# Attention backward on one core: the planner's greedy work order gives way to a fixed cyclic table

## The chip, the cores and the metric

One core of one Trainium2 chip runs the kernel. The metric is the device time of the whole program in microseconds (us); smaller is better. The core's engines are named as the profile names them: PE (TensorE, matrix products; PEld is its weight load), DVE (VectorE), ACT (ScalarE), POOL (GpSimd) and SP (SyncE, which here does nothing but issue transfers). All large transfers go through SP's one queue, all small ones through POOL's. One program stands for each engine, and each engine goes through its own in order: an instruction whose inputs are not there holds up everything behind it on that engine.

## The reference

```python
def _fwd_reference(q, k, v):            # q: 32 x 32 heads x 4 x 128, k and v: 32 x 4 heads x 2048 x 128, bf16
    k = jnp.repeat(k, 8, axis=1)
    v = jnp.repeat(v, 8, axis=1)
    scores = jnp.einsum("bhqd,bhkd->bhqk", q, k) * D ** -0.5
    p = softmax(scores, axis=-1)
    return jnp.einsum("bhqk,bhkd->bhqd", p, v)

def reference(q, k, v, grad_out):
    out, vjp = jax.vjp(_fwd_reference, q, k, v)
    return (out, *vjp(grad_out))        # out, dq, dk, dv
```

It is the forward pass of grouped attention (eight query heads share a key head) and its gradients to q, k and v. For a batch, four key heads with 2048 keys each are read (2 MB of k and 2 MB of v) and gradients of the same sizes are written (2 MB of dk and 2 MB of dv); q, grad_out, out and dq are 32 KB each.

## The kernel before, in words

The 32 batches are independent. With 8 heads x 4 queries, the 32 query rows of each of the four key heads fill the 128 partitions, so that one batch is worked on as a whole. The work of a batch is cut into **units**, made by `units_of` (L125) and turned into instructions by `emit` (L468); the names are those of the code:

- `LQ` loads q and grad_out (POOL's queue, L473 and L475); `LK` and `LV` load one head of k or v, 512 KB each (SP's queue, L481).
- `QT`, `KT`, `VT` (L484, L485, L495) transpose q, grad_out and blocks of k and v on PE, eight 128x128 blocks in a unit; `QTe`, `KTe`, `VTe` copy the result from PSUM to SBUF, on ACT (L463) or DVE (L466).
- `S` (L506) makes scores; `MX` (L513, DVE) the running maximum; `EX` (L522, ACT) the exponentials; `L` (L526, L528) the sums and their reciprocals; `dop`, `qp`, `rs` (POOL, L531 to L538) the scaled small operands.
- `ET` (L546) transposes the exponentials, `O` (L557) makes the output, `Oe` evicts it and `Os` stores it; `DL` (L572) is the row sum of out times grad_out.
- `DP` (L506) makes the gradient of p, `DS` (L579, DVE) that of the scores; `DT` (L546) transposes it, `DQ` (L557) makes dq, `DQe` and `DQs` evict and store it.
- `DV` and `DK` (L594) make four quarters of dv and dk each; every quarter is evicted by two `DVe` or `DKe` (L599), on ACT or DVE, 128x1024 elements each; `DVs` and `DKs` (L603) store two halves of 1 MB through SP's queue, when all four quarters of a half are there.

So a batch gives SP twelve transfers: eight loads of 512 KB and four stores of 1 MB. PE does all its work in three forms: transposes (128x128), products tiled by columns (`S`, `DP`, `O`, `DQ`) and products tiled by rows (`DV`, `DK`).

PSUM is one tile of eight banks (L454); a unit holds one bank or a pair, and `bank_of` says which. SBUF tiles come from pools whose sizes stand in `CAP` (L36): 12 tiles of k, 11 of v, 9 and 6 of the transposed ones, 6 halves of output.

What stands behind what is decided on the host, before the program is built. `plan` (L201) replays the machine: an event queue with occupancies (`OCC`), an instruction-fetch term of PE (`pe_length`, L229) and a transfer queue. Whenever an engine is free in this replay, `begin` (L287) takes the ready unit with the smallest due time, which is `b * PERIOD + DUE[name][i]` plus a correction of its own for batches 0, 1, 29, 30 and 31 (L134). Evictions go to ACT or DVE, whichever ends first (L388 to L403); banks are taken as they are free (`banks_for`, L261); SP takes a store when one is ready, and two loads behind each store if there are any (L378 to L387). The resulting list is emitted in its order (L606), and so each engine's program is the greedy replay's order frozen.

```python
        when = b * PERIOD + due[name[0]][i] + BY_BATCH.get(b, {}).get(name[0], [0.0] * 8)[i]
```

Of the kernel before, what the change touches and what calls it, by code (L numbers as in the profile page):

```python
# [18 lines left out]
NQ = 4  # L19
# [3 lines left out]
OCC = dict(QT=0.16, KT=0.45, VT=0.45, ET=0.45, DT=0.45, S=0.228, DP=0.228, O=0.23, DQ=0.23, DV=0.24, DK=0.24,  # L23
           MX=1.27, EX=1.11, L=0.5, DL=0.28, DS=1.21, dop=0.4, qp=0.4, rs=0.3,
           c16=(0.60, 0.48), c32=(1.135, 0.905), q16=(0.27, 0.165), o32=(0.28, 0.27))
# [3 lines left out]
FETCH, QUEUE, FIRST, EVERY = 2.35, 64, 705, (768, 1024)  # L29
SWITCH = 0.06  # L30
MODE = dict(S=1, DP=1, O=1, DQ=1, DV=2, DK=2)
LAG = dict(PE=0.21, ACT=0.13, DVE=0.13, POOL=0.13)
ISSUE = dict(LQ=1.5, Os=0.75, DQs=0.75)
SERVICE = dict(LQ=0.19, LK=1.287, LV=1.287, DVs=2.574, DKs=2.574, Os=0.18, DQs=0.18)
DMA_LAT, AGAIN, LOAD_LAG, STORE_LAG, AHEAD, HEAD = 2.1, 0.35, 1.4, 1.7, 3.3, 0.8
CAP = dict(q=4, et=2, dt=2, k=12, v=11, kt=9, vt=6, out=6, e=2, ds=2)  # L36
PERIOD = 38.14
FIRST_LQ, EVERY_LQ = -121.38, 29.52
DUE = dict(
    LQ=[2], LK=[-32.2, -26.2, -23.3, -21.6], LV=[-13.6, -7.1, -12.8, -13.3], QT=[379.6], QTe=[276.9],  # L40
    KT=[-1.5, -10.9, 87.6, 39.5, -176.9, 28.1, -28.4, 222.7],
    KTe=[175.1, 41.5, 163.9, 367.8, 163, 50, 155.9, -312],
    VT=[-443.5, -82.7, -68.7, -188.9, 19.6, -41.4, -1.1, 323.7],
    VTe=[323.5, -134.3, -108.5, 190.8, -22.8, 143.9, 133.3, 364.7], S=[219.2, -491.6, -275.5, -226.2],
    MX=[-66.7, -116.8], EX=[-189, 16.2], L=[-9.8], dop=[55.8], qp=[-129], rs=[335.3], ET=[-631.9, -72.5],
    ETe=[86.4, 62.9], DT=[12.5, -272.2], DTe=[309.7, 80.5], O=[-58.1, -99.1, 16, 18.9], Oe=[60.7],
    Os=[-204.4], DQ=[104.1, 202.1, 189, -53.5], DQe=[11.6], DQs=[-172.1], DL=[14.9],
    DP=[-151.2, 118.2, -290.9, -95.2], DS=[-316.3, -308.3], DV=[-207.6, -55.7, -6.3, 43.4],
    DVe=[81.8, 244.9, 385.7, 166.5, -349.8, 322.2, 15.6, -40.9], DVs=[-108.9, -1.7],
    DK=[121.5, 185, -172.9, -271.1], DKe=[-24.1, 266.2, 294.9, 637.6, 226.6, 68.8, 378.6, 377.2],  # L50
    DKs=[-91.7, -100.4], efree=[310.1], dsfree=[486.2])
BY_BATCH = {
    0: dict(
    LQ=[53.8], LK=[-46.7, -73.2, -9.4, 6.9], LV=[13.1, 18.5, 18.8, 15.6], QT=[-121.3], QTe=[47.3],
    KT=[15.3, 74.1, 73.1, 45.5, -16.9, 20.1, -24.7, 39.2],
    KTe=[-10.3, 8.3, -0.5, 105.5, -65.1, -15.8, 55.4, 112.3],
    VT=[-9.5, 90.4, -4, -1.5, -53.8, -108.2, 108, 87.5],
    VTe=[-36.8, 47.8, 91.1, -127.6, -61.7, 66, 33.3, 37.7], S=[-6.5, 81, -111.4, 11.8], MX=[-4.8, -20],
    EX=[-1.9, -137.8], L=[8.9], dop=[-22.9], qp=[-43.4], rs=[35.7], ET=[-69.5, 54.5], ETe=[-179.3, -52.4],
    DT=[-51.2, 43], DTe=[-15.6, -78.7], O=[81, 101.9, -91.5, -62.9], Oe=[-58.8], Os=[-12.5],  # L60
    DQ=[-18.6, -27.7, -55.8, 6.9], DQe=[-129.4], DQs=[97.5], DL=[-106.2], DP=[-151.9, 22.3, 64.8, -72.9],
    DS=[-134.9, -50.8], DV=[-74.8, -53.3, 57.5, -36.7], DVe=[-1, 106.4, 57, 43.6, -36.6, 34.7, -86, -71],
    DVs=[126.4, 45.7], DK=[43.2, -113.3, 21.5, 33.8],
    DKe=[-18.2, -92.2, 46.3, 4.7, 26.1, -42.9, -41.3, -115.6], DKs=[-7.5, -5.4], efree=[-40.9],
    dsfree=[-36.7]),
    1: dict(
    LQ=[-49.8], LK=[-3.6, -3.2, 18.8, 9.7], LV=[21.2, 3, 31.9, 21.4], QT=[145.1], QTe=[57.1],
# [57 lines left out]
def units_of(b, due):  # L125
    out, seen = [], collections.Counter()

    def add(name, eng, deps, opens=(), closes=()):
# [6 lines left out]
        if name[0] == "LQ":  # L135
            when = max(when, FIRST_LQ + EVERY_LQ * b)
# [499 lines left out]
```

## Time and profile before

| what | us |
|---|---|
| median of 6 runs (729.24 to 744.25) | 732.16 |
| the profiled execution's own time | 738.41 |
| its span, from the first instruction to the last | 736.6 |
| PE busy / DVE busy / ACT busy / POOL busy | 613.8 / 580.1 / 587.6 / 110.4 |
| bytes moved | 274.72 MB, mean 373 GB/s |
| SP's queue (q1), share of 16 engines' span | 94.5% |

The durations used below come from the profiled execution, which is 6.25 us over the median of the runs. "Busy" of PE counts pipelined products from their start to their modelled end and says little about how much more PE could do. "issue" in a wait is time in which the engine waited for nothing that the profile shows. q8 is the queue through which instructions are fetched.

### The profile page before, as it was taken

The page shows a single profiled execution, that of the slowest core. Times are in us where ns is not written, and L with a number is a line of the kernel's source. Part 1 is how long each engine was busy: PE and PEld are TensorE (multiplying, and loading weights), DVE is VectorE, ACT ScalarE, POOL GpSimd, SP SyncE. Part 2 cuts the span into 40 slices and gives each one's busy share as a digit, 9 for nine tenths or more (in the row PEclk, how much of TensorE's full clock was granted, in tenths as well). Part 3 has the DMA queues.
Part 4 walks back from the last instruction along what each step waited for, and adds up shares of the span by engine and source line. Part 5 has one row for each costly group of instructions (what it writes and reads, how often), then busy time and mean ns, then how long its engine had stood idle before and what let it go on. Part 6 is the DMA issues. An engine that isn't in the chain of part 4 may idle for free.

```text
span 736.6 us, 32366 instructions
## 1 busy us (share of the span) xinstructions
PE 613.8 (83%) x14400; PEld 459.6 (62%) x14400; DVE 580.1 (79%) x777; ACT 587.6 (80%) x920; POOL 110.4 (15%) x230
## 2 busy tenths in 40 slices
PE   5888988889888879888887997878878888788884
PEld 4666666666666656666666665656656666566663
DVE  1887888788887779888787896878868888867884
ACT  3787988889888788879888886778867888868784
POOL 2111101111111111111111110111101111101010
PEclk9999999999999999999999999999999999999997
DMA  9979999999999999999999999999999999999956
GB/s 345 393 303 352 330 414 394 409 387 381 388 413 401 362 401 365 391 391 372 415 411 412 343 411 402 341 387 367 373 387 350 360 398 372 402 351 377 397 211 258
DMA packets 75915, 274.72 MB, mean 373 GB/s; under 512 B 8192, under 2 KB 8192, under 8 KB 75776
## 3 DMA queue, kind: packets, MB, share of 16 engines
q1 hardware_dynamic: 71680, 268.46, 94.5%
q0 software_dynamic: 4096, 4.20, 1.7%
q8 instruction: 112, 1.84, 1.0%
q14 instruction: 27, 0.22, 0.1%
HBM read 136.31 MB, written 136.31 MB: 370 GB/s over the span
## 4 chain that ended last, share of the span: by engine, by line
PE 52%; ACT 22%; issue 12%; DMA 6%; DVE 5%; POOL 0%; POOLq 0%; DVEq 0%; ACTq 0%
PE psum L495 28%; PE psum L506 8%; PE psum L594 7%; PE psum L557 6%; ACT dk_sb L599 5%; ACT e_sb L522 5%; ACT dv_sb L599 4%; DMA k_sb<-in_k_dram 4%; ACT vt_sb L463 4%; DVE ds_sb L579 3%; PE psum L546 3%; DMA out_dram<-dv_sb 1%; ACT kt_sb L463 1%; ACT et_sb L463 1%; DMA go_sb<-in_grad_out_dram 1%
## 5 line engine op out<-in xcount | busy, mean ns | idle before, releaser
L599 DVE CAST dk_sb<-psum 128x1024 bf16<-128x1024 f32 x124 | 149.0, 1222 | 45.3 <-PE psum L594 41.8
L495 PE MATMUL psum<-ident,k_sb 128*128 128x128 bf16 x2048 | 153.2, 224 | 21.6 <-issue 9.4
L599 ACT CAST dv_sb<-psum 128x1024 bf16<-128x1024 f32 x153 | 154.7, 1032 | 15.2 <-PE psum L594 13.5
L495 PE MATMUL psum<-ident,v_sb 128*128 128x128 bf16 x2048 | 154.0, 224 | 14.5 <-issue 7.2
L495 PEld LDWEIGHTS <-v_sb 128*128 128x128 bf16 x2048 | 126.0, 100 | 49.4 <-issue 40.5
L599 ACT CAST dk_sb<-psum 128x1024 bf16<-128x1024 f32 x132 | 131.1, 1028 | 28.9 <-PE psum L594 28.4
L495 PEld LDWEIGHTS <-k_sb 128*128 128x128 bf16 x2048 | 124.6, 100 | 43.7 <-issue 28.6
L463 ACT COPY vt_sb<-psum 128x512 f32<-128x512 f32 x190 | 110.1, 594 | 44.0 <-PE psum L495 43.3
L599 DVE CAST dv_sb<-psum 128x1024 bf16<-128x1024 f32 x103 | 125.2, 1220 | 24.1 <-PE psum L594 22.3
L463 ACT COPY kt_sb<-psum 128x512 f32<-128x512 f32 x181 | 107.2, 600 | 29.9 <-PE psum L495 26.3
L579 DVE SCALAR_TENSOR_TENSOR ds_sb<-psum,delta,e_sb 128x1024 bf16<-128x1024 f32 x64 | 82.0, 1281 | 13.6 <-PE psum L506 13.3
L594 PE MATMUL psum<-qp_sb,ds_sb 32*128 32x128 bf16 x2048 | 60.3, 217 | 25.4 <-issue 10.4
L522 ACT ACTIVATE e_sb<-psum,m 128x1024 bf16<-128x1024 f32 x64 | 72.1, 1128 | 1.0 <-DVE mjunk L513 1.0
L594 PE MATMUL psum<-dop_sb,e_sb 32*128 32x128 bf16 x2048 | 58.0, 217 | 11.7 <-issue 4.7
L594 PEld LDWEIGHTS <-ds_sb 32*128 32x128 bf16 x2048 | 35.5, 92 | 47.2 <-issue 34.4
L557 PE MATMUL psum<-k_sb,dt_sb 128*32 128x128 bf16 x2048 | 47.7, 225 | 13.2 <-issue 11.9
L513 DVE TENSOR_SCALAR_CACHE_REDUCE mjunk<-psum,m 128x1024 bf16<-128x1024 f32 x32 | 41.1, 1284 | 21.1 <-PE psum L506 19.7
L594 PEld LDWEIGHTS <-e_sb 32*128 32x128 bf16 x2048 | 34.6, 92 | 36.0 <-issue 25.0
L466 DVE COPY kt_sb<-psum 128x1024 bf16<-128x1024 bf16 x75 | 50.5, 688 | 7.8 <-PE psum L495 4.5
L568 POOL DMA_DIRECT2D out_dram<-dq_sb x32 | 17.4, 545 | 241.5 <-DVE dq_sb L566 159.2
L534 POOL TENSOR_SCALAR qp_sb<-q_sb,rinv 128x128 bf16<-128x128 bf16 x32 | 11.7, 367 | 277.9 <-DVE rinv L528 180.5
L506 PE MATMUL psum<-vt_sb,qdt_sb 128*32 128x512 bf16 x512 | 49.0, 395 | 4.5 <-issue 2.3
(75 smaller groups left out, 650.9 us busy)
## 6 DMA issues: line engine op xcount, KB each, us to landing
k_sb<-in_k_dram SPq DMA_DIRECT2D x128, 512.0 KB, 10.0
v_sb<-in_v_dram SPq DMA_DIRECT2D x128, 512.0 KB, 10.3
out_dram<-dv_sb SPq DMA_DIRECT2D x64, 1024.0 KB, 9.7
out_dram<-dk_sb SPq DMA_DIRECT2D x64, 1024.0 KB, 9.0
q_sb<-in_q_dram POOLq DMA_DIRECT2D x32, 32.0 KB, 6.2
go_sb<-in_grad_out_dram POOLq DMA_DIRECT2D x32, 32.0 KB, 6.1
out_dram<-o_sb POOLq DMA_DIRECT2D x32, 32.0 KB, 6.4
out_dram<-dq_sb POOLq DMA_DIRECT2D x32, 32.0 KB, 5.7
```

Source lines behind the costliest of these rows:

```text
L463: nc.scalar.copy(out=out.rearrange("p c d -> p (c d)").bitcast(FP32), in_=in_.rearrange("p c d -> p (c d)").bitcast(FP32))
L466: nc.vector.tensor_copy(out=out, in_=in_)
L495: nc.tensor.transpose(out=ps[:, j, :], in_=t[x, h][:, 8 * i + j, :], identity=ident[:])
L506: nc.tensor.matmul(t[name, i][r, QW * w:QW * w + QW], lhsT=t["qdt"][:, side, r], rhs=t[x, h, i][:, CPQ * w:CPQ * w + CPQ, :], start=True, ...
L513: nc.vector.tensor_scalar(out=junk[:], in0=t["S", i][:], scalar1=-scale, scalar2=t["m"][:] if i else None, op0=ALU.mult, op1=ALU.min, accu ...
L522: nc.scalar.activation(out=t["e"][:, 2 * QW * i:2 * QW * i + 2 * QW], in_=t["S", i][:], func=ACT.Exp, bias=t["m"][:], scale=scale, accum_o ...
L546: nc.tensor.transpose(out=ps[:, j, :], in_=src[:, P * c:P * c + P], identity=ident[:])
L557: nc.tensor.matmul(t[name][r, 0:D], lhsT=t[xt, c // 8][:, c % 8, r], rhs=t[x, h][:, c, :], start=(c == 0), stop=(c == C - 1), tile_positio ...
L568: nc.gpsimd.dma_start(out=(o_r if name == "Os" else dq_r)[b], in_=t["o" if name == "Os" else "dq"][:])
L579: nc.vector.scalar_tensor_tensor(out=t["ds"][:, w], in0=t["DP", i][:], scalar=t["dl"][:], in1=t["e"][:, w], op0=ALU.subtract, op1=ALU.mult)
L594: nc.tensor.matmul(accs[h // 2][:, w:w + P], lhsT=t[lhs][r, P * c:P * c + P], rhs=t[rhs][r, :], start=True, stop=True, tile_position=(32 * ...
L599: copy(out=t[name[:2], "out", g][:, :, CPQ * i:CPQ * i + CPQ, :].rearrange("p h c d -> p h (c d)"), in_=t[name[:2], i][g][:].rearrange("p ...
```

## The change

The emitting code is the same to the letter (it only stands 69 lines higher: L495 becomes L426, L594 L525, L599 L530, L603 L534). What is replaced is how the list of units is made.

- `DUE` and the greedy replay go. Every unit has a place, `b * PERIOD + PLACE[name][i]` with PERIOD 21.3, and the list is the units sorted by place. The first two and the last three batches add shifts of their own.
- Who evicts is fixed by a table too (`ENGINE`, with `SWAP` for the five special batches).
- `plan` then goes through that list once, in order, and keeps times for each engine only to choose PSUM banks: the bank that comes free first.
- `CAP`: k 12 to 15, v 11 to 8, kt 9 to 8, vt 6 to 7; the rest is as before (small tiles had 4 buffers and have 4).
- `units_of` names the small tiles (qdt, rinv, dop, qp, rs, o, dq, dl) as resources, for this replay alone.

```diff
-CAP = dict(q=4, et=2, dt=2, k=12, v=11, kt=9, vt=6, out=6, e=2, ds=2)
-PERIOD = 38.14
-DUE = dict(
...
+CAP = dict(q=4, k=15, v=8, qdt=4, kt=8, vt=7, e=2, rinv=4, dop=4, qp=4, rs=4, et=2, dt=2, o=4, dq=4, dl=4, ds=2, out=6)
+PERIOD = 21.3
+PLACE = dict(
+    LQ=[-56.5568], LK=[-15.8907, -21.6263, -20.5047, -1.9095], LV=[-4.4505, 3.0463, -9.9868, 0.7178], QT=[-9],
...
+    22.5016, 21.6813, 25.005, 25.1674], DVs=[38.288, 41.6553], DK=[27.0554, 29.6814, 35.9041, 36.9241], DKe=[28.8067,
+    28.3557, 30.2326, 30.8423, 36.4058, 37.6717, 37.8885, 37.5117], DKs=[51.0221, 53.9145], gfree=[32.8019],
...
+ENGINE = dict(
+    QTe="D", KTe="DADADAAD", VTe="ADDADAAD", ETe="AA", DTe="AA", Oe="D", DQe="A", DVe="AADAADAD", DKe="ADAAADAD")
+SHIFT = {
...
+def placed(n_batches):
+    tail = {n_batches + b: b for b in SHIFT if b < 0}
+    out = []
+    for b in range(n_batches):
+        seen = collections.Counter()
+        special = tail.get(b, b)
+        for u in units_of(b):
+            name = u.key[1]
+            i = seen[name]
+            seen[name] += 1
+            u.at = b * PERIOD + PLACE[name][i] + (SHIFT[special][name][i] if special in SHIFT else 0.0)
+            if len(u.eng) == 2:
+                u.on = ENGINE[name][i]
+                if special in SWAP and SWAP[special].get(name, "-" * 16)[i] == "x":
+                    u.on = "D" if u.on == "A" else "A"
+                u.on = "ACT" if u.on == "A" else "DVE"
+            else:
+                u.on = next(iter(u.eng), "")
+            out.append(u)
+    return sorted(out, key=lambda u: u.at)
+
+def plan(n_batches):
+    order = placed(n_batches)
...
+    for u in order:
...
+        for r in sorted((r for r in u.opens if r[1] == "ps"), key=lambda r: -r[3]):
+            best, at = None, None
+            for i in range(0, BANKS, r[3]):
+                if any(holds[j] for j in range(i, i + r[3])):
+                    continue
+                when = max([now] + free[i:i + r[3]])
+                if r[3] == 1 and not holds[i ^ 1]:
+                    when += 1e-3
+                if best is None or when < best - 1e-12:
+                    best, at = when, i
+            bank_of[r] = at
...
+    return order, bank_of
```

What the two programs hold, engine by engine, follows from their lists:

| | before | after |
|---|---|---|
| SP, a batch in the middle | store, 2 loads, store, 2 loads, store, 2 loads, store, 2 loads | dk, v, dk, v, dv, k, dv, k, v, k, v, k |
| ACT: 128x1024 evictions of dv and dk / copies to kt, vt, et, dt | 285 / 435 | 319 / 377 |
| DVE: the same | 227 / 205 | 193 / 263 |
| changes of PE's form of work | 745 | 838 |
| SP behind the last load | 9 stores | 9 stores |

## The prediction

> **What bounds the kernel now.** First the slices and the queues of the page. DMA is all but full everywhere, and yet the rate moves between 303 and 415 GB/s:
>
> ```profile
> PE   5888988889888879888887997878878888788884
> DMA  9979999999999999999999999999999999999956
> GB/s 345 393 303 352 330 414 394 409 387 381 388 413 401 362 401 365 391 391 372 415 411 412 343 411 402 341 387 367 373 387 350 360 398 372 402 351 377 397 211 258
> ...
> q1 hardware_dynamic: 71680, 268.46, 94.5%
> q0 software_dynamic: 4096, 4.20, 1.7%
> q8 instruction: 112, 1.84, 1.0%
> ```
>
> So the transfers bound the kernel, but not at their best: at 412 GB/s, which seven of the 40 slices reach within 1%, 274.72 MB take 667 us, 70 less than the span of 736.6. Where these lie is told by the stages (columns: us, PE, PEld, DVE, ACT and POOL busy with instructions, PE clock, DMA share, GB/s):
>
> ```profile
> 40.00:100.00 60.00, 51.71 (x1271) 38.86 (x1270) 49.75 (x63) 50.36 (x81) 10.22 (x21) 0.97 0.88 335
> 100.00:330.00 230.00, 196.74 (x4709) 146.36 (x4709) 188.64 (x251) 192.85 (x307) 35.45 (x73) 0.99 1.01 391
> 330.00:560.00 230.00, 195.63 (x4603) 145.98 (x4596) 188.10 (x256) 185.32 (x289) 35.93 (x73) 0.98 1.00 382
> 560.00:700.00 140.00, 117.01 (x2716) 87.42 (x2705) 109.33 (x149) 111.36 (x171) 17.33 (x36) 0.96 1.00 381
> 700.00:736.60 36.60, 23.43 (x634) 17.04 (x632) 22.72 (x27) 23.39 (x36) 3.44 (x7) 0.87 0.60 234
> ```
>
> A batch moves 274.72 / 32 = 8.585 MB. From 100 to 700 us pass 89.9 + 87.9 + 53.3 = 231.1 MB, that is 26.9 batches at 22.3 us each; at 412 GB/s one takes 20.8. Why the queue falls short is told by what SP waited for:
>
> ```profile
> SPq L603 <- DVE dk_sb L599: 211.0, 39, 14.0
> SPq L603 <- ACT dv_sb L599: 120.4, 36, 6.0
> SPq L481 <- PE psum L557: 60.3, 24, 6.6
> SPq L603 <- DVE dv_sb L599: 34.7, 10, 5.7
> SPq L603 <- ACT dk_sb L599: 19.9, 5, 10.1
> ```
>
> SP stands before a store and waits for evictions for 386 us by these rows, and for 60 before a k load whose tile the dq products still read. Meanwhile the queue eats its lead. I took each transfer's issue and landing from the trace: of the loads issued with over 8 us of transfers ahead (134), each landed 0.01 us later than 1.25 us behind its predecessor; with 4 to 5 us (20) it was 0.74 us later, with 6 to 7 (41) 0.17. Stores (2.5 us each) lose 0.2 to 0.4 at any lead, 1.6 when the queue had run dry. Last the chain:
>
> ```profile
> PE 52%; ACT 22%; issue 12%; DMA 6%; DVE 5%; POOL 0%; POOLq 0%; DVEq 0%; ACTq 0%
> ```
>
> It runs over PE and ACT, not over transfers: the evictions that SP waits for are late because PE's and ACT's orders make them late. The "issue" in it is of one kind mostly:
>
> ```profile
> PEld L495 <- issue: 69.1, 161, 2.2
> PEld L594 <- issue: 59.4, 119, 2.8
> ```
>
> PE's program has 28,800 instructions, q8 brought 112 packets: one for 256. Counted along PE's starts, 52 long gaps (64 us in all) lie at the same place of a block of 256, and each ends 1.4 us after a q8 packet did. After such a gap the next packet starts 3.7 us later (median), takes 0.95, and 1.4 pass: a block that is limited by fetching takes 6.1 us, and the mean block of the whole run 6.36. A batch has 900 instructions, 3.52 blocks: **PE cannot go below about 21.4 us a batch** at the queue's present depth, close to the 20.8 of the transfers.
>
> **The change, part by part.**
>
> *SP's order.* No transfer is added or removed. In the lists of batches 3 to 28, a dv store stood on average 2.6 transfers behind its last eviction and now stands 6.1 behind (never under 5); a dk store 2.0 and now 9.8; a k load stood 2.1 transfers behind the dq that frees its tile and now 7.8 (15 tiles instead of 12), a v load 21 behind the o that frees its tile and now 12.5 (8 tiles instead of 11); k is loaded 5.5 MB of transfers ahead of its first use instead of 3.2. So SP should find its data ready, and the 386 + 60 us of waiting shrink to what keeps the queue from overfilling. What is late next is PE: with the queue deep, PE's fetch floor decides. I take 21.6 us a batch, the 21.4 and 0.2 for blocks that stop for other reasons as well: 26.9 x (22.3 - 21.6) = 18.8 us gained. Bounds: 20.8 us, as in the best slices, gives 40; no gain, 0.
>
> *Start, 0 to 100 us.* 21 loads stood before the first store, now 22, nearly in the same order. Then four stores in a row (two dk of batch 0, two dv of batch 1) stood before the next k load; now a load stands between nearly every two. 40 to 100 us carries 335 GB/s, 20.1 MB; at 365, halfway to the 391 of the next stage, it takes 55: 5 gained. Bounds: 0 (only v has fewer tiles, 8 instead of 11) and 9 (391).
>
> *Tail.* Nine stores follow the last load in both lists, 22.5 us of transfers in a stretch of 36.6, at PE clock 0.87; the chain of the last batch through EX, DP, DS, DK and eight evictions stays. k of batch 31 is loaded before v of 30 now. I take 1 us gained; from 5 lost to 8 gained.
>
> *Evictions.* ACT: 34 more of 1.03 us and 58 fewer of 0.60, 28 fewer qdt copies of 0.27, 6 fewer small ones of 0.4: -10 us. DVE: 58 more of 0.69, 34 fewer of 1.22, 28 more qdt of 0.29, 6 more of 0.35: +9. Against 587.6 and 580.1 us busy that is nothing, and both idle 20%.
>
> *PE's forms.* 93 more changes of form. The next unit starts 0.20 us after the last weight load, within transposes it is 0.056: 93 x 0.14 = 13 us. I cost it at nothing, since a block that waits for its fetch hides it: PE's starts without waits sum to 543 us (transposes 262, changes of form 146, tiled products 135), 17.0 a batch; of its 22.3 us, 2.0 are gaps for fetches (64 / 112 x 3.52) and 3.3 other waits. Without that cover it costs 13, which I keep for the upper end.
>
> *Banks.* Which bank a unit gets changes; the waits of PE on evictions of dk and dv in the profile (5.3, 3.9, 2.3, 1.3, 1.2) sum to 14 us, so this is between -14 and +14; I take 0, as the rule of taking the earliest free bank stays.
>
> *POOL.* The same DMAs and three small operations a batch; `dop` now precedes `qp`, its use in `DV` comes first. It is busy 110 us of 736: nothing.
>
> Sum: 18.8 + 5 + 1 = 25 us. Against the profiled execution (738.41, of that 1.8 outside the span) that makes 713; that execution was 6.25 over the median of the runs shown, so I set the 25 against 732.16: **707 us**.
>
> [...] The page's share of busy DMA (97.2% by the three rows) would leave 20 us at most, the GB/s leave 70. [...]
>
> **Rivals.**
>
> *A, the forecast (0.55)*: SP stops waiting, PE's fetch sets 21.4 to 22.0 a batch. Own range 693 to 722.
>
> *B, slower (0.16)*: SP no longer holds the queue back, and a deep queue delays the fetch. Blocks that began with 9 to 14 us in the queue (41) lasted 7.08 us, with 7 to 9 (33) 6.14. If 60% of the blocks begin so deep instead of 38%, the 112 blocks take 0.22 x 0.94 x 112 = 23 us more, with start and tail 6 less: 749. It decides from a mean block of 6.4 us on. Against it: the depth may follow from a slow PE rather than cause it, and a slower PE makes stores late, which empties the queue.
>
> *C, no change (0.15)*: the evictions stay as late as now because ACT's and PE's chain takes 22.3 us in any order; SP's wait returns at stores that merely stand later, and the first 100 us give 5: 727 to 738. For it: the chain has 74% on PE and ACT. Against: both have a fifth of waits left.
>
> *D, more (0.14)*: fetches hide behind PE's waits and the transfers alone set 20.9 us a batch (410 GB/s): 26.9 x 1.4 = 38, start 8, tail 4: 682.
>
> **How the numbers follow.** The likeliest case is A, 707. D lies about 682, half of B above 749, so 684 to 742 leaves out some 0.07 at each end; B's middle is near the upper one. About 1% is what a measurement of this kernel tells from no change: faster than 725 are D and nearly all of A, together 0.68 and a little of C: 0.70; within 1% most of C: 0.14; slower B: 0.16.
>
> **What would show it.** SP's waits at the store line on evictions well under 200 us (from 386); 40 to 100 us above 350 GB/s and the stages between 100 and 700 us near 398; "issue" waits of PE's weight loads no smaller than now, and more of the chain on issue. ACT and DVE busy within 15 us of before. Wrong would be: a mean block of 6.4 us or more (B); SP's store waits still above 300 us (C); stages at 408 or more with "issue" nearly gone (D).

## The result and the profile after

The changed kernel takes 739.07 us at the median of 10 runs (732.75 to 744.68), the kernel before 731.99 in the 20 runs beside them. The ratio is 1.0098, with a 95% interval of 1.0063 to 1.0133: it is 1% slower, 7 us, where 25 us less had been forecast. Its profiled execution took 739.52 us, with a span of 737.8. The profiled execution of before was a long one (738.41, 6 us over its median), so the two profiles differ by 1 us only; the pair shows where time moved and understates how much.

First the same lines of the page as shown of before:

```profile
PE   6798887878878888889878898987989878888884
...
DMA  9999999999999999999999999999999999999957
GB/s 345 408 403 400 380 411 360 369 386 351 399 347 373 396 371 384 367 403 343 396 371 394 397 338 410 367 397 405 367 409 349 404 374 343 356 329 366 409 237 283
...
q8 instruction: 112, 1.84, 0.9%
...
PE 65%; ACT 10%; issue 10%; DMA 8%; DVE 6%; SPq 0%; DVEq 0%; POOLq 0%; ACTq 0%; POOL 0%
```

SP's queue carries the same 71680 packets and 268.46 MB, and q8 the same 112 packets of instructions. The slices behind the first are better for a while (408, 403, 400, where 393, 303, 352 stood), later ones are not. The chain of waits has gone from ACT (22% to 10%) to PE (52% to 65%). The stages say it in numbers (columns as before: us, PE, PEld, DVE, ACT and POOL busy with instructions, PE clock, DMA share, GB/s):

```profile
40.00:100.00 60.00, 52.61 (x1267) 38.87 (x1253) 51.15 (x74) 49.08 (x74) 10.11 (x21) 1.00 1.02 395
100.00:330.00 230.00, 192.68 (x4497) 142.17 (x4497) 180.33 (x259) 182.45 (x269) 34.98 (x70) 0.98 0.98 377
330.00:560.00 230.00, 196.45 (x4583) 146.54 (x4581) 185.42 (x269) 187.18 (x279) 35.98 (x72) 0.98 0.99 384
560.00:700.00 140.00, 121.18 (x2881) 90.69 (x2879) 117.08 (x168) 113.27 (x169) 19.36 (x39) 0.98 0.96 364
700.00:737.80 37.80, 24.96 (x662) 18.77 (x659) 23.38 (x32) 25.41 (x37) 3.81 (x8) 0.88 0.67 263
```

40 to 100 us carries 395 GB/s instead of 335. From 100 us on the rate is lower than before in two stages of three (377 for 391, 364 for 381). Followed by the exponentials of single batches: those of batch 2 start at 55.8 us instead of 62.0, 6.2 earlier; those of batch 31 at 710.5 instead of 708.3, so the 29 batches between lost 8.4 us; from there to the end it takes 27.3 us instead of 28.3. -6.2 + 8.4 - 1.0 is the 1.2 us by which the spans differ. **In this pair the start gained what was hoped for, and the middle gave back more.** The middle's loss is the firmer of the two: between batches 4 and 27 one batch takes 22.63 us, against 22.25 in the profile of before. (Another profiled execution with the old order of work, that of the run on banks below, took 732.35 us and 22.08 us a batch; against that the middle loses 0.55.) The size of the start's gain is not settled: in that other execution the exponentials of batch 2 start at 59.7 us, and in the profiles of the later runs made from the new kernel with its order of loads they start at 55.8 to 61.3.

SP's waits after, by what they were for:

```profile
SPq L534 <- ACT dk_sb L530: 150.1, 32, 13.6
SPq L412 <- PE psum L426: 88.7, 51, 4.3
SPq L412 <- PE psum L525: 84.8, 31, 4.5
SPq L534 <- ACT dv_sb L530: 72.4, 31, 4.6
SPq L412 <- PE psum L488: 41.9, 10, 7.5
SPq L412 <- PE psum L437: 22.6, 32, 1.6
SPq L534 <- DVE dk_sb L530: 14.2, 4, 6.4
SPq L534 <- DVE dv_sb L530: 9.9, 3, 4.3
```

At the store line (L534, before L603) the 386 us became 150.1 + 72.4 + 14.2 + 9.9 = 246.6. At the load line (L412, before L481) waits for a tile to come free became 88.7 + 84.8 + 41.9 + 22.6 = 238.0, where before L557, L594, L506 and L495 stood with 60.3 + 14.3 + 14.1 + 10.2 = 98.9; the last three are these rows of before:

```profile
SPq L481 <- PE psum L594: 14.3, 11, 3.1
SPq L481 <- PE psum L506: 14.1, 19, 1.4
SPq L481 <- PE psum L495: 10.2, 20, 1.2
```

The sums are 484.6 after and 484.9 before (with the smaller rows 528.6 and 528.0): SP waits as long as it did, only for something else. Nor did the queue become deep, as the forecast had it. The last number of these lines of the page is the median time in us from the issue of a transfer to its landing, first before, then after:

```profile
k_sb<-in_k_dram SPq DMA_DIRECT2D x128, 512.0 KB, 10.0
out_dram<-dv_sb SPq DMA_DIRECT2D x64, 1024.0 KB, 9.7
```

```profile
k_sb<-in_k_dram SPq DMA_DIRECT2D x128, 512.0 KB, 8.5
out_dram<-dv_sb SPq DMA_DIRECT2D x64, 1024.0 KB, 7.9
```

At nearly the same rate a transfer lands sooner, so less stands ahead of it in the queue than before.

Last, PE's own waits, the greatest that name something:

```profile
PEld L426 <- issue: 79.2, 169, 1.9
PEld L525 <- issue: 44.6, 102, 2.3
...
PE psum L426 <- ACT vt_sb L394: 14.5, 26, 0.6
...
PE psum L477 <- ACT dk_sb L530: 14.0, 27, 0.5
...
PE psum L426 <- DVE ds_sb L510: 11.7, 20, 0.7
...
PE psum L525 <- ACT et_sb L394: 9.2, 23, 0.7
```

The four kinds of wait on ACT and DVE sum to 49.4 us; before, the greatest of the kind had 7.5 and 6.4:

```profile
PEld L546 <- DVE ds_sb L579: 7.5, 23, 1.2
...
PE psum L594 <- DVE l L526: 6.4, 17, 0.4
```

All rows of PE's products that name ACT or DVE sum to 39.3 us before and 68.4 after. The four kinds come 20 to 27 times each, that is about once a batch. One such place, in the timeline of after (columns: start, us, engine, line, what; in brackets the idle time before it and what ended it):

```profile
354.53 0.59 ACT L394 COPY et_sb<-psum 128x512 f32<-128x512 f32 x1 [0.50 <-PE psum L477]
...
355.01 0.59 ACT L394 COPY dt_sb<-psum 128x512 f32<-128x512 f32 x1
355.17 0.23 PE L525 MATMUL psum<-qp_sb,ds_sb 32*128 32x128 bf16 x3 [0.39 <-ACT et_sb L394]
...
355.66 0.38 PE L525 MATMUL psum<-qp_sb,ds_sb 32*128 32x128 bf16 x13 [0.25 <-ACT dt_sb L394]
...
356.57 0.61 PE L477 MATMUL psum<-ident,e_sb 128*128 128x128 bf16 x8 [0.54 <-ACT dk_sb L530]
```

The last `DK` unit of batch 14 needs two pairs of banks, and in each pair one that a copy frees, `ETe` of batch 15 and `DTe` of batch 14; ACT makes them one behind the other, and PE stands before the first bank (0.39 us), again before the second (0.25), and then before `ET` for the bank that the dk eviction on ACT frees (0.54): 1.18 us between 354.8 and 356.6.

An account of PE between batches 4 and 27, worked out from the starts of its weight loads (the usual step from one to the next counts as work, what is beyond it as a wait, and a wait that falls on the same place of a block of 256 instructions as a fetch gap), us a batch:

| | before | after |
|---|---|---|
| transposes and tiled products | 8.20 + 2.57 | 7.94 + 2.61 |
| changes of form (23.8 and 27.0) | 4.73 | 5.38 |
| fetch gaps (54 and 38 of them in 23 batches) | 2.58 | 1.52 |
| other waits | 4.16 | 5.19 |
| a batch | 22.25 | 22.63 |

So PE's work grew by 0.4, fetch gaps fell by 1.06, and the other waits, for banks and data in the main, took back 1.03 of that. The sum says where the time lies, not which of these parts caused the others. By the same account two other executions with the old order of work (the runs on banks and on 15 tiles of k below, both 22.08 us a batch) have fetch gaps of 2.3 and 2.2 and other waits of 4.3 and 4.4, so a difference of 0.3 between two profiles means little.

### The profile page after: what moved, and what is told of

The parts are those of the page before. It is cut to its first block, busy times and chain, and to the rows that moved or that the text cites. A ratio compares the mean times of both kernels' runs of the same rounds, so it can differ in the third digit from the quotient of the medians.

```text
span 737.8 us, 32599 instructions
## 1 busy us (share of the span) xinstructions
PE 615.6 (83%) x14400; PEld 458.7 (62%) x14400; DVE 582.0 (79%) x835; ACT 581.6 (79%) x862; POOL 112.7 (15%) x230
## 3 DMA queue, kind: packets, MB, share of 16 engines
q1 hardware_dynamic: 71680, 268.46, 94.0%
## 4 chain that ended last, share of the span: by engine, by line
PE 65%; ACT 10%; issue 10%; DMA 8%; DVE 6%; SPq 0%; DVEq 0%; POOLq 0%; ACTq 0%; POOL 0%
PE psum L426 31%; PE psum L488 10%; PE psum L525 9%; PE psum L437 9%; PE psum L477 7%; ACT dk_sb L530 4%; DVE ds_sb L510 3%; DMA out_dram<-dv_sb 3%; DMA k_sb<-in_k_dram 2%; DMA v_sb<-in_v_dram 2%; ACT e_sb L453 2%; ACT dt_sb L394 2%; ACT vt_sb L394 1%; DVE mjunk L444 1%; DVE dv_sb L530 1%
## 5 line engine op out<-in xcount | busy, mean ns | idle before, releaser
L426 PE MATMUL psum<-ident,v_sb 128*128 128x128 bf16 x2048 | 161.1, 223 | 39.0 <-ACT vt_sb L394 14.5
L426 PEld LDWEIGHTS <-v_sb 128*128 128x128 bf16 x2048 | 123.3, 99 | 88.7 <-issue 71.0
L530 ACT CAST dk_sb<-psum 128x1024 bf16<-128x1024 f32 x161 | 157.8, 1024 | 9.2 <-PE psum L525 9.0
L530 ACT CAST dv_sb<-psum 128x1024 bf16<-128x1024 f32 x158 | 155.7, 1024 | 11.8 <-PE psum L525 8.4
L426 PE MATMUL psum<-ident,k_sb 128*128 128x128 bf16 x2048 | 148.9, 222 | 6.6 <-DMA k_sb<-in_k_dram 5.1
L530 DVE CAST dk_sb<-psum 128x1024 bf16<-128x1024 f32 x95 | 113.6, 1221 | 31.1 <-PE psum L525 26.5
L426 PEld LDWEIGHTS <-k_sb 128*128 128x128 bf16 x2048 | 119.0, 99 | 28.5 <-issue 8.2
L530 DVE CAST dv_sb<-psum 128x1024 bf16<-128x1024 f32 x98 | 119.4, 1220 | 16.7 <-PE psum L525 16.4
L397 DVE COPY vt_sb<-psum 128x1024 bf16<-128x1024 bf16 x128 | 87.3, 684 | 36.7 <-PE psum L426 32.6
L394 ACT COPY vt_sb<-psum 128x512 f32<-128x512 f32 x128 | 77.5, 608 | 41.6 <-PE psum L426 39.3
L397 DVE COPY kt_sb<-psum 128x1024 bf16<-128x1024 bf16 x126 | 84.0, 683 | 19.6 <-PE psum L426 18.2
L394 ACT COPY kt_sb<-psum 128x512 f32<-128x512 f32 x130 | 74.5, 610 | 23.8 <-PE psum L426 23.0
L525 PE MATMUL psum<-qp_sb,ds_sb 32*128 32x128 bf16 x2048 | 61.7, 217 | 29.1 <-ACT et_sb L394 9.2
L525 PEld LDWEIGHTS <-ds_sb 32*128 32x128 bf16 x2048 | 34.6, 92 | 50.0 <-issue 36.2
L525 PE MATMUL psum<-dop_sb,e_sb 32*128 32x128 bf16 x2048 | 61.0, 218 | 4.2 <-issue 1.4
L477 PE MATMUL psum<-ident,e_sb 128*128 128x128 bf16 x512 | 38.9, 219 | 16.2 <-ACT dk_sb L530 14.0
L462 POOL TENSOR_SCALAR dop_sb<-go_sb,rinv 128x128 bf16<-128x128 bf16 x32 | 19.8, 618 | 212.4 <-DVE rinv L459 209.9
L437 PE MATMUL psum<-vt_sb,qdt_sb 128*32 128x512 bf16 x512 | 47.7, 403 | 3.0 <-issue 1.9
```

Source lines behind the costliest of these rows:

```text
L394: nc.scalar.copy(out=out.rearrange("p c d -> p (c d)").bitcast(FP32), in_=in_.rearrange("p c d -> p (c d)").bitcast(FP32))
L397: nc.vector.tensor_copy(out=out, in_=in_)
L426: nc.tensor.transpose(out=ps[:, j, :], in_=t[x, h][:, 8 * i + j, :], identity=ident[:])
L437: nc.tensor.matmul(t[name, i][r, QW * w:QW * w + QW], lhsT=t["qdt"][:, side, r], rhs=t[x, h, i][:, CPQ * w:CPQ * w + CPQ, :], start=True, ...
L462: nc.gpsimd.tensor_scalar(out=t["dop"][:], in0=t["go"][:], scalar1=t["rinv"][:], scalar2=None, op0=ALU.mult)
L477: nc.tensor.transpose(out=ps[:, j, :], in_=src[:, P * c:P * c + P], identity=ident[:])
```

## The experiments

"The new kernel" is the changed one, "the old" the one before. All ratios are to the old kernel, run beside each; a distance to the new kernel is the difference of two ratios (its own is 1.0098), and is uncertain by some 4 us where a run has ten executions and by some 7 where it has four. The theories whose numbers the expectations give are these, in short: the first puts the loss into the new order of PE's work (1a: into its 93 more changes of form) and lets SP's new order keep a gain; the second puts it into the transfers' new order, or says that transfers which are issued earlier gain nothing. Later texts say themselves what they set against what.

### One half of the change alone

**SP's new order and the tile counts, with the old order of work** (the list of SP's transfers is merged anew into the old order of the other engines):

```diff
+SP_ORDER = """
+LK0.1 LK0.0 LK0.2 LK0.3 LV0.2 LV0.1 LK1.0 LV0.0 LV0.3 LK1.3 LK1.2 LK1.1 LV1.2 LK2.1 LV1.3 LK2.2 LV1.1 LK2.0
...
-    k_pool, v_pool = pool("kp", CAP["k"]), pool("vp", CAP["v"])
+    k_pool, v_pool = pool("kp", 15), pool("vp", 8)
...
     order, bank_of = plan(B)
+    order = with_loads(order, dict(K=15, V=8))
```

> The old work order of PE, ACT, DVE and POOL with the new kernel's order of transfers on SP and its tile counts for k and v (15 and 8). Theory 1 (the order of the compute engines sets the pace of a batch, 22.2 us in the old order and 22.6 in the new, and SP's order only matters in the first 100 us): a batch keeps 22.2 us, the start gains some 6, so 722 to 732. Theory 2 (SP's new order is what costs, since its stores stand behind more loads and go out late): it follows the new kernel, 737 to 742.

Measured: 740.29 us, ratio 1.0074 [1.0023, 1.0126]. Loads landed 20 us ahead of their first use, and a batch took 22.44 us. SP's waits at the store line fell to 312 us (386 before) and those at the load line on PE rose to 178, the same exchange as in the new kernel. The transfers' new order, with its tile counts, gains nothing on the old order of work and costs 0.7%, as the second theory had it.

**The new order of work, with SP's old order** (the same edit, with the old list, in the new kernel; tiles 15 and 8):

```diff
+SP_ORDER = """
+LK0.1 LK0.0 LK0.2 LK0.3 LV0.0 LV0.3 LK1.0 LV0.2 LK1.1 LV0.1 LK1.3 LK1.2 LV1.1 LK2.0 LV1.0 LV1.3 LK2.1 LK2.2
...
+    order = with_loads(order, dict(K=15, V=8))
```

> The other half: the new work order of the compute engines with the old order of transfers on SP, with 15 tiles of k and 8 of v. Theory 1 (compute order sets the pace): a batch keeps 22.6 us and the gain of the start is lost, 737 to 748. Theory 2 (SP's order costs): it follows the old kernel, 729 to 735.

Measured: 763.21 us, ratio 1.0394 [1.0328, 1.046]. The first exponentials start at 21.3 us instead of 15.3, and a batch takes 22.89 us instead of 22.63. The new order of work needs its own order of loads; the halves do not add up (0.7% and 3.9% alone, 1.0% together), so neither has a price of its own in the sum.

**The old order, with the banks chosen by the new replay:**

```diff
-    order, bank_of = plan(B)
+    order, _ = plan(B)
+    bank_of = banks_in_order(order)
```

> The old kernel with one thing of the change alone: PSUM banks chosen by the new in-order replay on the old list. Theory 1 (form changes and in-order waits of the new table cost, not the choice of banks): within 4 us of before, 728 to 736. Rival (the new choice of banks makes products wait for evictions): 737 or more, with PE's waits on evictions of dk and dv above the 14 us of before.

Measured: 732.95 us, 1.0014 [0.9969, 1.006]. How the banks are chosen is worth nothing that can be measured, on the old order; on the new one it was not tried.

**The old kernel with 15 tiles of k and 8 of v, SP's old order kept:**

```diff
-    k_pool, v_pool = pool("kp", CAP["k"]), pool("vp", CAP["v"])
+    k_pool, v_pool = pool("kp", 15), pool("vp", 8)
...
+    order = with_loads(order, dict(K=15, V=8))
```

> The old kernel with every engine's order kept, SP's too, and 15 tiles of k and 8 of v as in the new one: a k load no longer waits for the dq products of the batch before (60 us of SP's waits). Theory 1 (compute sets the pace): 728 to 736, with SP's wait for those products gone and longer waits before the stores. Theory 2 (SP's waits cost): 700 to 722.

Measured: 733.98 us, 0.9989 [0.9951, 1.0026]. Its SP waits:

```profile
SPq L655 <- DVE dk_sb L651: 231.5, 32, 15.1
SPq L655 <- ACT dv_sb L651: 120.2, 39, 7.4
SPq L655 <- DVE dv_sb L651: 34.1, 12, 5.7
SPq L655 <- ACT dk_sb L651: 18.1, 4, 7.2
...
SPq L533 <- PE psum L547: 9.5, 14, 3.6
```

The 60.3 us before a k load whose tile the dq products still read are gone, and the waits before stores (L655) grew from 386 to 404. (Three tiles of v fewer brought 19 us of new waits before v loads.) All of SP's waits together fell from 528 to 494.5 us, and the time stayed. Together with the run on SP's new order, this is the plainest evidence against the forecast's main step.

### Less or more work, one engine at a time

**Fewer bytes** (the second head of the second half of dk and dv is not sent, in the new and in the old kernel: 33.6 MB of 274.7):

```diff
-            nc.sync.dma_start(out=(dv_r if name == "DVs" else dk_r)[b, g],
-                                in_=t[name[:2], "out", g][:].rearrange("p h c d -> p h (c d)"))
+            w = slice(0, 2 - g)
+            nc.sync.dma_start(out=(dv_r if name == "DVs" else dk_r)[b, g][:, w, :],
+                                in_=t[name[:2], "out", g][:, w].rearrange("p h c d -> p h (c d)"))
```

> The new kernel, storing a quarter less: of the second half of dk and of dv the second head is left out (it is computed and evicted, but not sent), so a batch moves 7.5 MB instead of 8.6 and needs some 2.5 us less of transfers. Theory 1 (PE, ACT and DVE set the pace, transfers follow): within 8 us of the new kernel, 731 to 742, the tail alone gaining 2.5. Theory 2 (transfers set the pace): up to 27 x 2.5 = 68 less, 671 to 690. Theory 3 (both, each stalling the other): between, 700 to 725.

> The old kernel, storing a quarter less (the second head of each second half of dk and dv is left out): 68 us of transfers fewer. In the new kernel that took 23 us off. If transfers weigh in both through PE's instruction fetches: 18 to 28 less, 704 to 715. If the old kernel was bound by its queue as such: 40 us less or more, below 692. If by compute alone: under 8 less.

Measured: new 715.74 us, 0.9764 [0.9681, 0.9847], 24 us below the new kernel; old 719.25, 0.9756 [0.968, 0.9832], 18 below the old. At 412 GB/s the bytes left out would take 81 us: a quarter of that comes back. In the new kernel a batch falls from 22.63 to 21.79 us; of the 0.84 PE's fetch gaps give 0.66 (1.52 to 0.86) and its other waits 0.15 (5.19 to 5.04). So in the new kernel most of it comes as instructions that reach PE sooner. In the old one the profile does not tell: its batch takes 21.83 us and its fetch gaps 2.15, but the two other executions of the old order with all bytes have 22.08 and 2.2 to 2.3.

**Less evicted as well** (in the new kernel that sends fewer bytes, the 8 of 16 evictions of a batch that fill second halves of dv and dk evict half as much):

```diff
+            if g:
+                copy(out=out[:, 0, CPQ * i:CPQ * i + CPQ, :].rearrange("p (h c) d -> p h (c d)", h=2),
+                     in_=src[:, :, 0:QW // 2])
+            else:
+                copy(out=out[:, :, CPQ * i:CPQ * i + CPQ, :].rearrange("p h c d -> p h (c d)"), in_=src)
```

> The run before with evictions cut as well: the eviction of each second half of dk and dv (half of the sixteen 128x1024 evictions of a batch) copies 512 columns instead of 1024, so dk and dv are left out in part; PE's products stay. It takes some 8 x 0.5 us of a batch from ACT and DVE together, 2 us from each. Theory 1a (PE's own work and order set the pace): no more than 10 us below the run before. Theory 1b (PE's waits for evictions set it, since PSUM has eight banks): 27 x 1 to 2 us less than the run before, 27 to 54.

Measured: 714.34 us, 0.9743 [0.9678, 0.9809]. DVE's busy time fell from 580.9 to 510.3 us and ACT's from 581.6 to 549.1 against the run before, and the time by 1.4 us, inside the uncertainty. In this kernel with fewer bytes, the evictions that SP names in its longest wait do not set the pace.

**More transposes** (one of the eight of each k and v unit is done twice, in the new and in the old kernel):

```diff
-            for j in range(8):
+            for j in [0, 1, 2, 3, 4, 5, 6, 7, 7]:
```

> The new kernel with one of the eight transposes of every k and v unit done twice: 512 x 2 instructions more on PE, 16 x 0.056 = 0.9 us of a batch, 29 us in all. Theory 1a (PE sets the pace): 760 to 770. Theory 1b (waits take it up): 739 to 748.

> The old kernel with one of the eight transposes of every k and v unit done twice, 29 us more work for PE; the same edit made the new kernel 25 us slower. Theory 1a (PE set the pace before the change as well): 753 to 760. Theory 2 (before, SP's waits for stores and the queue's short lead set the pace, and PE had slack): 732 to 742.

Measured: new 764.03 us, 1.0431 [1.0332, 1.0531], 24 us over the new kernel; old 752.32, 1.0247 [1.0153, 1.0342], 18 over the old. 512 more products at 0.056 us from start to start are 28.7 us of PE, so 85% and 63% of it show, each uncertain by a quarter. They are also 1024 more instructions, which four more packets brought (page of the new one; 112 without the edit):

```profile
q8 instruction: 116, 1.90, 0.9%
```

**Less of DVE** (the second of the two row maxima of a batch is left out, in the new and in the old kernel):

```diff
+            if i:
+                return
```

> The new kernel without the second of the two row maxima (the maximum over keys 1024 to 2047 is left out; the exponentials are shifted by that of the first half). It takes 1.28 us of a batch from DVE and from the way between scores and exponentials. Theory 1c (PE's order runs into that stretch with PSUM full, so its length is part of a batch's time): 20 to 35 us below the new kernel, 704 to 719. Theory 1a (PE's work in sum sets the pace, DVE has slack): within 8 us of the new kernel, 731 to 742.

> The old kernel with the same left out. Theory 1c: 20 to 35 us below the old kernel, 698 to 713. Theory 1a: 724 to 735.

Measured: new 733.46 us, 0.9996 [0.9959, 1.0032], 7 us below the new kernel; old 731.8, 0.9949 [0.9911, 0.9987], 4 below the old. DVE's busy time fell by 36 us in the new kernel (582.0 to 545.6) and by 40 in the old (580.1 to 540.3): about 20% and 9% show, each uncertain by a tenth.

Set side by side, no engine is *the* bound: the transfers give back a quarter of what is taken from them, DVE a tenth to a fifth, ACT and DVE in the evictions nothing, while transposes on PE cost two thirds or more of their time.

### PE's changes of form

**Five places moved by at most 0.41 us, so that units of one form stand together** (708 changes instead of 838):

```diff
-    QTe=[-8.7], KT=[3.6462, 1.6844, 5.905, 3.1839, -4.9499, 3.8925, 0.752, 7.1379], KTe=[6.1903, 3.7011, 7.2224,
-    4.9828, -3.781, 5.6021, 1.8065, 9.2289], VT=[9.3333, 12.7464, 12.7122, 12.1725, 23.3342, 19.8257, 21.6688,
-    29.8813], VTe=[12.271, 14.2038, 13.3178, 12.2885, 24.7313, 21.7914, 22.5082, 31.287], S=[9.0488, 9.0588, 10.2822,
+    QTe=[-8.7], KT=[3.6462, 1.6844, 5.905, 2.77, -4.9499, 3.8925, 0.752, 7.2131], KTe=[6.1903, 3.7011, 7.2224,
+    4.9828, -3.781, 5.6021, 1.8065, 9.2289], VT=[9.3333, 12.7464, 12.7122, 12.1725, 23.3342, 19.8072, 21.9456,
+    29.6807], VTe=[12.271, 14.2038, 13.3178, 12.2885, 24.7313, 21.7914, 22.5082, 31.287], S=[9.0488, 9.0588, 10.2822,
```

> The new kernel with five places of the table moved by 0.02 to 0.41, so that PE changes its form of work 708 times instead of 838 (before: 745); ACT's and DVE's orders are the same to the letter. Theory 1a (PE sets the pace and each change of form costs its 0.14 us in full): 130 x 0.14 = 18 us less than the new kernel, 719 to 724. Theory 1b (in-order waits between PE and the evictions set the pace and take up what PE saves): within 5 us of the new kernel, 734 to 743.

Measured: 731.11 us, 0.9969 [0.9926, 1.0012], 9 us below the new kernel and as fast as the old. It looked like the answer: the 1% had gone with the changes of form.

**The same five moves in batches 2 to 28 only:**

```diff
+MOVED = {("VT", 5): -0.0185, ("KT", 7): 0.0752, ("VT", 7): -0.2006, ("VT", 6): 0.2768, ("KT", 3): -0.4139}
...
+            if special in SHIFT:
+                u.at -= MOVED.get((name, i), 0.0)
```

> The run with fewer changes of form, but with the five places moved in batches 2 to 28 alone, so that the first and the last batches keep the new kernel's order: the new kernel was at the scores of batch 2 at 55.8 us, the old at 62.0, the run with the places moved everywhere at 60.6. If the start's gain lasts and the body takes 22.2 us a batch as there: 724 to 728. If what the start gains is lost again behind it: 729 to 734.

Measured: 732.81 us, 0.9976 [0.9934, 1.0018]. The gain lies in the middle batches, not in the start or the tail. Its profile (the fastest of ten executions, 727.65) has 22.02 us a batch. By the account of PE, changes of form take 4.4 us for 22.0 of them, where the new kernel has 5.38 for 27.0, and transposes 8.3 (7.94), since more steps stay among transposes; fetch gaps are 1.4 (1.52) and other waits 5.3 (5.19). So what these moves gained lies in PE's work, and its waits stayed. PE's rows that name ACT or DVE still sum to 59.4 us here: a kernel as fast as the old one keeps most of the waits that the new order brought (68.4, before 39.3).

**Further moves in batches 2 to 28: 669 changes, and with one more move 617:**

```diff
+MOVED = {("KT", 3): 0.2243, ("KT", 7): 0.0752, ("VT", 5): -0.0185, ("VT", 7): -0.2006, ("DP", 1): -0.2768, ("DV", 2): 0.5121, ("DK", 0): 0.8582}
...
+            if special not in SHIFT:
+                u.at += MOVED.get((name, i), 0.0)
```

The second of the two has `("VT", 0): 2.1683` beside these.

> The new kernel with seven places moved by at most 0.86 in batches 2 to 28: PE changes its form 669 times (new 838, old 745, the runs with five places moved 708). Theory 1a (PE sets the pace; of a change's 0.14 us about half came off the time in the earlier runs, 9 us for 130): 169 x 0.073 = 12 us below the new kernel, 725 to 729. Theory 1b (what came off there was the start or chance): 731 to 737.

> The same with one more place moved, a transposing unit of v by 2.2: 617 changes of form. Theory 1a: 221 x 0.073 = 16 us below the new kernel, 721 to 726. Rival: a unit moved by a tenth of a batch finds its bank taken and PE waits there, so nothing more is gained than at 669, or less.

Measured: 756.23 us, 1.0289 [1.0211, 1.0368], and 754.58, 1.0264 [1.0186, 1.0343]: fewer changes of form than in any kernel so far, and 2 to 3% slower than the old. Waits of PE in the first:

```profile
PEld L440 <- issue: 37.6, 56, 1.6
PE psum L440 <- ACT dk_sb L533: 30.0, 28, 1.5
```

The new wait is at `S` (L440, with three lines added to the new kernel's L437), once a batch and 1.1 us long, for the bank that a dk eviction on ACT frees. In the account of PE the changes of form fall to 4.08 us a batch and fetch gaps to 0.87, both lower than in the new kernel, and the other waits rise from 5.19 to 7.05. What seven moves of under 1 us saved in changes of form they lost, and more, to waits for banks and data.

**The old kernel with 131 moves within its order** (at most 2 us of the planner's time each; 745 changes become 610; banks by the replay):

```diff
+MOVES = """
+DP23.3>DP23.2 DP25.3>DP25.2 DP27.3>DP27.2 DP2.3>DP2.2 DP3.3>DP3.2 DP4.3>DP4.2 DP5.3>DP5.2 DP6.3>DP6.2
...
-    order, bank_of = plan(B)
+    order = grouped(plan(B)[0])
+    bank_of = banks_in_order(order)
```

> The old kernel with PE units moved by at most 2 us of the planner's time to stand beside others of their form: 610 changes instead of 745; ACT, DVE and SP keep their orders, banks come from the in-order replay, which by itself changed nothing. Theory 1a (PE sets the pace in the old kernel too): 135 x 0.073 = 10 us less, 719 to 724. Theory 2 (the old kernel waited on transfers and evictions, not on PE): 729 to 735, or slower by units that stand in a worse place.

Measured: 740.82 us, 1.0073 [1.0028, 1.0118]. A fifth fewer changes, and slower. By the account, what they saved went to waits: the waits other than fetch gaps are 5.1 us a batch, and 4.3 in the run on banks.

**The price of a change of form by itself** (four products with 8 columns a batch, with results that nobody reads, behind transposes of the old kernel: once in the column-tiled form, so that PE changes form and back, and once in the form of the transposes around them):

```diff
+                if j == 3 and x == "K" and i == 0:
+                    spot = psum[:, QW * at:QW * at + QW]
+                    nc.tensor.matmul(spot[0:32, 448:456], lhsT=ident[:, 0:32], rhs=ident[:, 0:8],
+                                     start=True, stop=True, tile_position=(0, 0))
```

```diff
+                    nc.tensor.matmul(spot[:, 448:456], lhsT=ident[:], rhs=ident[:, 0:8], start=True, stop=True)
```

> The old kernel with a product of 8 columns, tiled by columns, between the fourth and fifth transposing of the first half of each k head: 4 a batch, 256 changes of form more in all. By 0.14 us each that is 36 us of PE's time and 7 us for the products themselves. If added work of PE costs what the doubled transposes cost in the old kernel (63%): 22 to 30 us more than before. If changes of form hide in PE's waits: under 8 more.

> The same products in the form of the transposes: no change of form is added, 7 us of PE's time are. At 63%: 3 to 7 us more than before. If it comes out as slow as the run with the other form, the form costs nothing, and what costs is the product between the transposes.

Measured: 736.59 us, 1.0048 [1.0012, 1.0085], and 736.19, 1.005 [1.0014, 1.0085]. PE's line of the page, first with the other form, then with the same:

```profile
PE 629.0 (85%) x14528; PEld 464.2 (63%) x14528; DVE 580.6 (79%) x777; ACT 589.9 (80%) x920; POOL 109.9 (15%) x230
```

```profile
PE 611.1 (83%) x14528; PEld 458.5 (62%) x14528; DVE 580.3 (79%) x777; ACT 587.2 (80%) x920; POOL 109.9 (15%) x230
```

In the other form the step into the product is 0.200 us and the one out of it 0.110, in the same form 0.056 each: 0.20 us more for each of 128, 25 us in all. 256 more changes of form, and the time differs by 0.4 us, with some 4 us of uncertainty. What both cost alike is 3.6 us, for 256 more instructions. The account of PE shows where the 25 us went: fetch gaps are 2.4 us a batch with the same form and 1.6 with the other, 26 us less in 32 batches, and the other waits differ by 0.1. PE reached the end of a block later and waited less there for the next one. So in the old kernel changes of form are hidden, as the forecast had it. For the new kernel this was not tried. Its fetch gaps are shorter to begin with, and there the five moves' saving in work did show; so theory 1a falls for the old kernel and stays open for the new.

What more PE work costs, then, goes with how many *instructions* it has and not with its time: per 256 instructions 6 us (more transposes, new kernel), 4.5 (the same, old), 3.6 and 3.5 (same form, other form), each uncertain by 2 to 3 us, while the PE time added per 256 is 7.2, 7.2, 7.2 and 32 us. The mean block of 256 instructions lasts 6.4 us in the whole run. That goes with a PE that is paced, on the average, by the blocks of its program as they arrive: in the old kernel the fetch gaps took up the 25 us of the other form, which brings no more instructions than the same form (2.4 to 1.6 us a batch), and did not take up the doubled transposes, which are more instructions (2.5 a batch with them). That is an inference from four runs; a run in which the same work has fewer instructions, which would test it directly, was not made. The count of q8's packets goes with it: 1024 more instructions brought four more (112 to 116), and 256 more brought one (113, in either form).

## Why the prediction was wrong, point by point

- *SP's order, 18.8 us gained.* This is the step that failed: "So SP should find its data ready, and the 386 + 60 us of waiting shrink to what keeps the queue from overfilling. What is late next is PE". In its place a batch became 0.4 us longer, which over 23 batches is a loss of 9, and SP's new order by itself cost 0.7% (1.0074). It failed in two ways. First, SP did not find its data ready: the 386 + 60 us did not shrink to little, the same 485 us stood at loads as well as at stores. The distances ("now stands 6.1 behind") were counted in a list that is ordered by the planner's clock, and across engines such a distance does not say when things happen in the running program. By transfer, SP waited 114 us on PE before v loads, though they "now" stood 12.5 behind the product that frees their tile, and under 1 us before the change. Second, SP's waiting was taken for a loss that the time would show. With 15 tiles of k the wait for the dq products went and SP's waits fell by 33 us in sum, and the time stayed (0.9989).
- The reading ahead of it, "So the transfers bound the kernel, but not at their best", fell too: a queue that is 94% occupied gave back a quarter of the time of the bytes taken from it. The new order did make transfers early: loads land 21 us ahead of their first transposing, where k landed 4.0 us and v 5.6 ahead before. The old order of work did not need them earlier (20 us ahead with a ratio of 1.0074). Nor was the queue deep, on which the 21.6 us a batch was to rest: from issue to landing a k load took 8.5 us instead of 10.0.
- *Start, 5 us gained:* 6.2 in this pair of profiles; its size is not settled, since other executions reach batch 2 at 59.7 us in the old order and at up to 61.3 in the new. *Tail, 1 us gained:* right, 1.0 from the last batch's exponentials on, although the stage behind 700 us is 1.2 longer.
- *Evictions, nothing:* right. ACT is busy 581.6 us (forecast 10 below 587.6), DVE 582.0 (forecast 9 above 580.1), and taking evictions away changed nothing that could be measured.
- *PE's forms, nothing, at most 13 us:* right in the old kernel, where it was measured by itself and the fetch gaps hid it (25 us of changes for 0.4 us). In the new order it is doubtful: PE's work grew by 0.43 us a batch there, 12 us over 27 batches, and the five moves, which took changes of form away, gained 9 us with PE's waits as they were. They moved units as well, so this points to the forms and does not show them to be the loss.
- *Banks, nothing:* right for the choice of banks, tried on the old order (1.0014). What was missed is that the *order* decides when a bank is asked for: PE's waits for banks and data grew by 1.03 us a batch. The forecast had no term for them; it had taken them with the 14 us of the old order, in which the greedy replay starts a unit only when its bank is free. Whether these waits cost time by themselves is not shown, since the run with the five moves keeps them and is as fast as the old kernel.
- *The fetch floor, 21.4 us a batch, "no smaller than now":* as a floor it stands, no run went under 21.79 us a batch. As what comes next it was wrong: fetch gaps became smaller (2.58 to 1.52 us a batch), while PE's other waits grew by as much and less stood in the transfer queue. The mean block, 6.36 us before and 6.39 after (the first and the last left out), is only the batch divided by 3.52 and can't tell a cause.
- *Of the signs named:* 40 to 100 us above 350 GB/s came (395), the stages near 398 did not (377, 384, 364), the store waits fell to 246.6, between the two marks. "issue" waits of PE's weight loads did not stay (173.4 to 167.6 us) and the chain has less on issue, not more (12% to 10%); ACT and DVE stayed within 15 us.
- *The rivals:* C was nearest, "the evictions stay as late as now because ACT's and PE's chain takes 22.3 us in any order", with the wait back at loads rather than at stores. B had the sign but not the mechanism: the queue was not deeper but shallower (10.0 to 8.5 us from issue to landing), and fetch gaps shrank; its mark, a mean block of 6.4 us, was all but reached (6.39) by any batch that is so much longer. D did not come.

What is settled: SP's new order does not bring the gain, alone it costs 0.7%, though the new order of work needs it (3.9% without); the loss is in the middle batches; PE's work there grew by 0.4 us a batch, and what its fetch gaps gave back (1.06) went to other waits (1.03), many of them at places that come about once a batch. That small moves in the order matter is shown by the runs in which they gained 1% or cost 2 to 3%; the 3% lay in a new wait at `S`, the gain, by the account, in fewer changes of form. What stays open: whether the changes of form are the whole of the new kernel's 1%, what would have to go for it to pass the old, and why SP's new order costs 0.7% with the old order of work. No version tried that does the whole work is faster than the old kernel by more than the measurement can tell; the five moves come nearest, 0.9969 [0.9926, 1.0012].

## What to carry to other kernels

An engine that only issues transfers can have waits to spare, whoever is named in them (here 528 us of 737, before a new order and after it): before a forecast removes such a wait, ask who would go faster for it. Where several engines are 80 to 95% occupied, add or remove work of one at a time; the share that shows in the time (here 63 to 85% for transposes, 22 to 30% for bytes, 9 to 20% for the maxima and nothing for evictions) ranks them as no view of busy time does. And when a greedy order, which looks at what is free, is replaced by a fixed table, count for each unit which bank it will ask for and which copy must have ended, since seven moves of under 1 us cost 3% here by a new wait of PE at `S`, about once a batch (28 times, 30.0 us).

## What the runs showed of the hardware that was not expected

- A product in another tile form between transposes takes PE 0.200 us to get into and 0.110 to get out of, against 0.056 each in the same form; in the old kernel 25 us of this added nothing to the time (736.59 against 736.19 us), and the gaps at which PE waits for instructions became 26 us shorter.
- With 12% fewer bytes on the transfer queue, the gaps at which PE waits for instructions fell from 1.52 to 0.86 us a batch in the new kernel; in the old one (2.2 to 2.6 with all bytes, 2.15 with fewer) the profiles do not tell.
- Landing 20 us instead of 4 to 6 ahead of use was worth nothing to the loads of this kernel with its old order of work (740.29 us, 1.0074).
